# Retention and two expert layers on one core: the retention slots of the first layer one step later, eight weight tiles converted singly

## The chip, the cores and the metric

The kernel runs on one core of one Trainium2 chip. The time is device microseconds (us) of one execution, given as the median of the runs. The engines are called as in the profile: PE (TensorE, matmuls), PEld (its weight loads), DVE (VectorE), ACT (ScalarE), POOL (GpSimd), SP (SyncE, which here only issues DMAs). A line such as L505 is a line of the kernel before the change.

## The reference

```python
for b in range(nb):                                   # retention, 12 blocks of 64 positions
    intra = einsum('bhic,bhjc->bhij', qb, kb) * Dmask
    intra = einsum('bhij,bhjd->bhid', intra, vb)
    inter = einsum('bhid,bhde->bhie', qb * lam_pow, kv_state)
    out[:, :, sl] = intra + inter
    kv_state = lam_block * kv_state + einsum('bhsd,bhse->bhde', kb * rev_pow, vb)
x = attn_out as 1536 tokens x 512
h = x @ w_in ; g = relu(h)**2 ; x = g @ w_out          # block 0: d_ff 2048
out = (sigmoid(x @ w_gate) * (x @ w_val)) @ w_out      # block 1: d_ff 1536
```

q, k, v and lam are float32, the five weight matrices are float64 in memory. Retention has 2 sequences of 768 positions, 8 heads of 64.

## The kernel before, in words

Retention works on chunks of 128 positions: 12 chunks, taken in pairs of one chunk of each sequence, (0, 6), (1, 7), up to (5, 11). Two pairs are done ahead of everything else. They give the first 512 tokens, with which block 0 starts at once; the other four pairs are worked into block 0, while it runs on the first 512 tokens, and give the other 1024 tokens, which block 0 handles afterwards.

**Block 0 on the first 512 tokens** has 16 steps, f = 0 to 15, one for each 128 rows of d_ff (`step_1`). A step has two halves on PE: `stage_a` (12 matmuls, L505), which multiplies the tokens by the weight tile in*f*, and `stage_b` (12 matmuls, L519), which multiplies the squared result of the step *before* by the weight tile out*f-1*. Below they are called A*f* and B*f*: PE's order is A0, A1, B0, A2, B1, A3, B2 and so on. Every float32 operand is split into a high and a low part that PE can multiply at full rate, and a product takes three groups of four matmuls: high by high, low by high (of the weights), high by low. So A*f* needs the high part of its weights (whi, ACT, L240) for the first four matmuls and the low part (wlo, DVE, L243) for the next four. The result of A*f* passes ACT three times (relu L536, square L537, high part gh L549) and DVE once (low part gl, L551) before B*f* can use it.

**Weights** come as float64. SP loads the raw words (`raw`, L149, 512 KB); ACT scales the high and the low word in two instructions (L163, L167), DVE shifts and adds (L174, L179), which leaves float32; later ACT and DVE split it (L240, L243), and SP stores the float32 tile to memory for the tokens that come later (L231). The tiles go in the order in0, in1, out0, in2, out1, in3, out2, in4, out3, in5, ... The first `SINGLE` of them are converted one by one (512 columns an instruction); the rest in couples, two tiles to one instruction of DVE and of the split. `PLAN` says what a step issues: "S" splits the next tile or couple, "A" scales, shifts and adds the next one, "a" and "b" are the two halves of such a conversion. The first S of a step stands ahead of stage_b, the rest behind it. A step that is not in the table has "SA". A step in `LATE` issues gl and the low part of its first S behind stage_b.

**Retention inside block 0.** A half step is one stage: half step 2f comes behind A*f*, half step 2f+1 behind B*f-1*. `SLOTS` gives a half step the scores of a chunk (16 matmuls, L360, then two masks on DVE, L386, and on POOL the decayed keys kd, L376, and queries qd, L368) or the output of a pair (96 matmuls, L412, L428, L440, then the state on DVE, L454, two copies to xr on ACT, L464; on POOL tt, L394). `LOADS` gives the half step at which SP is handed the load of a chunk's q and k (a "q" entry, L118 and L123) or k and v (a "v" entry, L127).

The order of each engine is that in which the program issues, and each engine keeps to it. SP is a queue as well: a DMA whose buffer or semaphore isn't free holds those behind it. Instructions that make the low and high parts of the 1024 other tokens (`combine_x`: xch L597, xcl L600, t L613) and of the combined weights (ah L687, al L693) are put at positions near the end of the sixteen steps; behind them PE goes on with L714 for the other 1024 tokens.

Of the kernel before, what the change touches and what calls it, by code (L numbers as in the profile page):

```python
# [14 lines left out]
TB = 512  # L15
WARM = 14
FILL = 10
SINGLE = 6
PLAN = {
    0: "SAaSb", 3: "SASA", 5: "SAA", 7: "SAA", 8: "SAA",  # L20
    10: "SAS", 11: "SS", 12: "S", 13: "", 14: "", 15: "",
}
LATE = (1,)

PAIRS = ((0, 6), (1, 7), (2, 8), (3, 9), (4, 10), (5, 11))
LEAD = 2
SLOTS = {
    3: ("scores", 2), 4: ("scores", 8), 6: ("out", 2),
    8: ("scores", 3), 9: ("scores", 9), 11: ("out", 3),
    13: ("scores", 4), 14: ("scores", 10), 16: ("out", 4),  # L30
    17: ("scores", 5), 18: ("scores", 11), 20: ("out", 5),
}
LOADS = {
    3: "q3", 4: "q10", 5: "v3", 6: "v9", 8: "q4", 9: "q11",
    10: "v4", 11: "v10", 12: "q5", 13: "q12", 14: "v5", 15: "v11",
}

MM = 0.2267
# [5 lines left out]
def retention_moe_kernel(  # L44
# [92 lines left out]
    order_1 += [(1, NF1 - 2, 1), (1, NF1 - 1, 1)]  # L137
    couples = [(key,) for key in order_1[:SINGLE]]
    couples += [tuple(order_1[n : n + 2]) for n in range(SINGLE, len(order_1), 2)]
    to_load = [key for couple in couples for key in couple]  # L140
# [62 lines left out]
    def several(n, name, dt=F32):  # L203
        return double(name, dt) if n == 2 else unit(name, dt).rearrange("p (n c) -> p n c", n=1)
# [13 lines left out]
    def couple_act():  # L218
        run(couple_ops())
# [15 lines left out]
    def couple_split():  # L235
        if not whole_t:
            return []
        keys, w = whole_t.pop(0)
        hi, lo = (several(len(keys), name, F32R) for name in ("whi2", "wlo2"))
        nc.scalar.copy(hi, w)  # L240
        for n, key in enumerate(keys):
            split_t[key] = hi[:, n], lo[:, n]
        return [lambda: nc.vector.tensor_tensor(out=lo, in0=w, in1=hi, op=ALU.subtract)]  # L243

    def weave(a, b):

        for i in range(max(len(a), len(b))):
            for ops in (a, b):
                if i < len(ops):
                    ops[i]()  # L250

    def run(ops):
        weave(ops, [])
# [10 lines left out]
    S = const.tile([P, 2, 4, 64], F32, name="S")  # L264
# [853 lines left out]
    def load(what, eng=nc.sync):  # L1118

        for x in what.split():  # L1120
            if x == "w":
                load_w(1)
            elif x[0] == "q":
                load_qk(int(x[1:]), eng)
            else:
                load_kv(int(x[1:]), eng)
# [34 lines left out]
    def step_1(f):  # L1161

        acc = stage_a(1, f)
        h = 2 * f
        masks = SLOTS.get(h, ("", 0))[0] == "scores"
        after = attend(h)
        gs, ops = split_g(elem(1, f, acc))
        if masks:
            after()
        if f not in LATE:  # L1170
            run(ops)
        if not masks:
            after()
        while rest:
            rest.pop()()
        plan = PLAN.get(f, "SA")
        lo = []
        if plan.startswith("S"):
            lo = couple_split()
            plan = plan[1:]  # L1180
        if f not in LATE:
            run(lo)
        if prev:
            stage_b(*prev.pop())
        after = attend(h + 1)
        if f in LATE:
            after()
            run(ops)
            run(lo)
            after = lambda: None  # L1190
        half_done = []
        for what in plan:
            if what == "S":
                run(couple_split())
            elif what == "a":
                first, second = couple_ops()
                first()
                half_done.append(second)
            elif what == "b":
                half_done.pop()()  # L1200
                run(couple_dve())
            else:
                couple_act()
                after()
                after = lambda: None
                run(couple_dve())
        after()
        prev.append((1, f, gs))
# [19 lines left out]
    T1 = (24 * NF1 - 12) * MM + 8 * SCORES + 4 * REST  # L1228
# [5 lines left out]
    with tc.manual_schedule():  # L1234
        load_lam()
        load("q6", nc.scalar)
        load("q0 q7 v0 v6 w q1 q8 v1 v7 w w w q2 w w q9")
        decays()
        warm_up(WARM)
        new_xr()  # L1240
        first, second = PAIRS[:LEAD]
        for c in first:
            att_scores(c)
        warm_up(FILL)
        for c in first:
            att_keys(c)
        run([op for c in first for op in att_mask(c)])
        att_uv(first)
        couple_act()
        att_state()  # L1250
        run(couple_dve())
        for c in (7, 1, 8):
            query(c)
        decayed()
        att_out(first)
        x_1 = att_x(first)
        for c in second:
            att_scores(c)
        lo_0 = couple_split()
        run([op for c in second for op in att_mask(c)])  # L1260
        run(lo_0)
        run(x_1)
        for c in second:
            att_keys(c)
        att_out(second)
        x_2 = att_x(second)
        couple_act()
        run(x_2)
        run(couple_dve())
        j_2, r_2 = couple_ops()  # L1270
        j_2()
        lo_1 = couple_split()
        r_2()
        shift_2, add_2 = couple_dve()
        shift_2()
        run(lo_1)
        add_2()
        load("v2 v8")
        att_uv(second)
        rest.append(att_state)  # L1280
        for c in (0, 6, 1, 7):
            qk_t.pop(c)
        for c in (0, 6, 1, 7):
            kv_t.pop(c)
        clock[0] = 0.0
        flush()


        keys = [(1, i, 0) for i in range(NF1 // 2)]
        prepare_a(keys[0], T1 - 2.0)  # L1290
        at(T1 - 20.0, lambda: load_a((1, 1, 0)))
        combine_x(1, [T1 + d for d in (-27, -25, -22.5, -20, -17.5, -15, -12.5, -10, -7, -4, -2)])
        for f in range(NF1):
            step_1(f)
        n_out = 24
        for k in range(3):
            at(T2 - 14.0 + k, lambda: load_w(1))
        for k in range(n_out):
            convert(T2 + 1.0 + k * (T3 - T2 - 4.0) / n_out)
        for f in range(NF1):  # L1300
            prepare_out(1, f, T2 + 24 * MM * f)
        uses = [use for i in range(NF1 // 2) for use in pair_in_1(i)]
        strassen(keys, uses, (None, lambda: close(1)))
        xc.clear()
        new_xr()
        for f in range(2):
            at(T3 - 24.0 + f, lambda f=f: load_units(2, f))
        at(T3 - 14.0, lambda: run(split_w(2, 0)))
        pair_out(1)


        for f in range(2, NF2):
            at(T3 + (36 * (f - 1) - 12) * MM - 8.0, lambda f=f: load_units(2, f))
        for k in range(3 * NF2 - n_out):
            convert(T3 + 2.0 + 3.6 * k)
        for i in range(NF2 // 2):
            sum_out_w(i, T4 - 64.0 + 9.0 * i)
        keys = [(2, i, u) for i in range(NF2 // 2) for u in range(2)]
        prepare_a(keys[0], T4)
        at(T4 - 28.0, lambda: combine_a((2, 0, 1)))  # L1320
        at(T4 - 20.0, lambda: load_a((2, 0, 1)))
        combine_x(2, [T4 - 46.0 + 3.5 * k for k in range(11)])
        for f in range(NF2):
            step_2(f)
        T6 = T5 + 6 * STEP
        by_unit_through_dram(1, T5 - 14.0, T5 - 7.0)
        through_dram(2, T5 - 4.0, T5 + 1.5)
        through_dram(3, T5 + 1.0, T5 + 6.5)
        through_dram(4, T5 + 6.0, T5 + 11.5)
        for n, load, pos in (  # L1330
            (0, -21.0, -13.0), (1, -12.0, -1.5), (2, -6.0, 4.0),
            (3, 1.0, 8.8), (4, 6.0, 13.5), (5, 11.0, 18.3),
        ):
            prepare_w(0, n, n, T5 + load, T5 + pos)
        for n, i, load, pos in (
            (0, 5, -12.5, -5.0), (1, 4, -7.5, -1.0), (2, 3, -3.0, 3.5),
            (3, 0, 1.0, 8.0), (4, 2, 6.0, 12.5), (5, 1, 10.0, 15.5),
        ):
            prepare_w(1, n, i, T6 + load, T6 + pos)
        by_unit_through_dram(2, T6 - 7.0, T6 + 5.0)  # L1340
        by_unit_through_dram(1, T6, T6 + 10.2)
        uses = [use for i in range(NF2 // 2) for use in pair_in_2(i)]
        strassen(keys, uses, (None, lambda: close(2)))
        blocks_out()
        flush()
        assert not agenda and not to_conv and not ready
# [62 lines left out]
```

## Time and profile before

| what | us |
|---|---|
| median of 3 runs | 582.85 (581.88 to 585.62) |
| profiled execution | 586.79 |
| its span, first to last instruction | 585.0 |
| PE busy in the span | 573.7 (98%) |
| DVE busy | 444.2 (76%) |
| ACT busy | 349.4 (60%) |
| mean granted TensorE clock | 0.990 of full speed |

The profiled execution is one run with the profiler on, a little slower than the median of the runs without it. The page gives shares of the whole span; what a change in one stage is worth has to be read in that stage. In the timeline a row has the start, the duration, the engine, the line and operation, the tiles, and in brackets how long the engine sat idle ahead of it and who ended that.

### The profile page before, as it was taken

To read this page: it belongs to the slowest core of one execution; us is meant where nothing else is said; L and a number is where in the kernel's file an instruction comes from. 1 tells how busy PE (TensorE), PEld (TensorE's weight loads), DVE (VectorE), ACT (ScalarE), POOL (GpSimd) and SP (SyncE) were. 2 spreads that over 40 slices of the span, in tenths; PEclk is the share of its full clock that TensorE was granted. 3 is DMA by queue.
4 is the path that set the end of the run, shared out by engine and by line. 5 is a ranking of instruction groups with operands and counts; after the bars stand their busy time and mean duration, and the time that the engine had idled before them with its cause. 6 is when DMAs were issued, how large, how long until landed. Compare 5 with 4: busy or idle time off the path is not lost.

```text
span 585.0 us, 8530 instructions
## 1 busy us (share of the span) xinstructions
PE 573.7 (98%) x3020; PEld 465.1 (79%) x3020; DVE 444.2 (76%) x637; ACT 349.4 (60%) x550; POOL 54.9 (9%) x52
## 2 busy tenths in 40 slices
PE   9988999999999999999999999999999999999996
PEld 5766878888888888888888888888878888878885
DVE  7886787798688866867556778884778877789974
ACT  3656688886465647676448665443554555485470
POOL 4344430000000000000000000012102210000000
PEclk9987999999999999999999999999999999999999
DMA  8998999501444497999994899994547668578671
GB/s 308 408 408 335 319 288 383 180 36 38 143 147 177 162 329 282 408 410 411 403 380 148 289 339 352 363 281 75 155 113 207 193 198 235 169 308 309 210 302 72
DMA packets 69226, 150.25 MB, mean 257 GB/s; under 512 B 6976, under 2 KB 15168, under 8 KB 69184
## 3 DMA queue, kind: packets, MB, share of 16 engines
q1 hardware_dynamic: 65312, 144.86, 68.2%
q0 software_dynamic: 3360, 3.93, 4.4%
q10 hardware_dynamic: 512, 0.92, 0.5%
q8 instruction: 23, 0.38, 0.3%
q14 instruction: 19, 0.16, 0.1%
HBM read 105.91 MB, written 42.21 MB: 253 GB/s over the span
## 4 chain that ended last, share of the span: by engine, by line
PE 87%; DVE 7%; ACT 2%; DMA 2%; issue 1%; DVEq 0%; SPq 0%; ACTq 0%
PE p L714 28%; PE p L505 18%; PE p L1105 15%; PE p L519 12%; PE p L1034 8%; DMA gr<-gs 2%; PE p L360 2%; PE p L440 2%; PE p L324 1%; DVE wlo L243 1%; DVE gq L901 1%; DVE at L386 1%; PE p L412 1%; PE p L428 1%; DVE c L728 1%
## 5 line engine op out<-in xcount | busy, mean ns | idle before, releaser
L714 PE MATMUL p<-xch,ah 128*128 128x512 f32 x280 | 109.9, 392 | 1.0 <-ACT s L723 0.5
L714 PE MATMUL p<-xcl,ah 128*128 128x512 f32 x280 | 109.1, 389 | 0.0
L714 PE MATMUL p<-xch,al 128*128 128x512 f32 x280 | 109.0, 389 | 0.0
L714 PEld LDWEIGHTS p<-xch,ah 128*128 128x128 f32 x280 | 52.5, 188 | 14.9 <-ACT s L723 3.2
L723 ACT COPY s<-p 128x512 f32<-128x512 f32 x60 | 35.1, 588 | 44.3 <-PE p L714 44.2
L714 PEld LDWEIGHTS p<-xch,al 128*128 128x128 f32 x280 | 52.6, 188 | 11.0
L714 PEld LDWEIGHTS p<-xcl,ah 128*128 128x128 f32 x280 | 52.6, 188 | 10.7
L728 DVE TENSOR_TENSOR c<-p,s 128x512 f32<-128x512 f32 x60 | 41.2, 687 | 23.2 <-PE p L714 23.2
L1034 PE MATMUL p<-gq,wq 128*128 128x512 f32 x252 | 57.7, 390 | 1.0 <-DVE wq L991 1.0
L1034 PEld LDWEIGHTS p<-gq,wq 128*128 128x128 f32 x252 | 47.1, 188 | 11.4 <-DVE wq L991 1.7
L163 ACT ACTIVATE j<-raw 128x512 f32<-128x512 f32 x68 | 45.5, 669 | 12.4 <-DMA raw<-in_w 6.6
L179 DVE CUSTOM_DVE_ANT_0 j<-j,r 128x1024 uint16<-128x1024 uint16 (+1 forms) x55 | 48.1, 874 | 6.2 <-DVE j L174 0.5
L1105 PE MATMUL p<-g2l,whi 128*128 128x512 f32 x128 | 49.8, 389 | 0.0
L1105 PE MATMUL p<-g2h,wlo 128*128 128x512 f32 x128 | 49.8, 389 | 0.0
L1105 PE MATMUL p<-g2h,whi 128*128 128x512 f32 x128 | 49.8, 389 | 0.0
L167 ACT ACTIVATE r<-raw 128x512 int32<-128x512 uint32 x68 | 45.1, 663 | 1.5 <-PE p L505 1.0
L505 PE MATMUL p<-xh,wlo 128*128 128x512 f32 x160 | 44.0, 398 | 1.4 <-DVE wlo L243 1.4
L505 PE MATMUL p<-xh,whi 128*128 128x512 f32 x160 | 44.5, 401 | 0.4 <-ACT whi L240 0.4
L505 PE MATMUL p<-xl,whi 128*128 128x512 f32 x160 | 43.6, 395 | 0.0
L662 POOL DMA_DIRECT2D as<-w x6 | 5.6, 926 | 364.3 <-DMA u<-w 292.9
L505 PEld LDWEIGHTS p<-xh,wlo 128*128 128x128 f32 x160 | 30.7, 192 | 8.5 <-DVE wlo L243 1.9
L505 PEld LDWEIGHTS p<-xh,whi 128*128 128x128 f32 x160 | 30.1, 191 | 7.5 <-ACT whi L240 0.8
(126 smaller groups left out, 1026.9 us busy)
## 6 DMA issues: line engine op xcount, KB each, us to landing
raw<-in_w SPq DMA_DIRECT2D x68, 512.0 KB, 7.6
w<-j SPq DMA_DIRECT2D x68, 256.0 KB, 7.3
u<-w SPq DMA_DIRECT2D x52, 256.0 KB, 5.8
a<-w SPq DMA_DIRECT2D x20, 512.0 KB, 4.0
g<-g SPq DMA_DIRECT2D x32, 256.0 KB, 3.7
g<-g SPq DMA_DIRECT2D x16, 512.0 KB, 7.6
kv<-in_kv SPq DMA_DIRECT2D x12, 512.0 KB, 7.9
gr<-gs SPq DMA_DIRECT2D x24, 256.0 KB, 5.5
```

Source lines behind the costliest of these rows:

```text
L163: lambda: nc.scalar.activation(j, t[:, :, 1].bitcast(F32), AF.Prelu, scale=2.0**-80 if flip else 2.0**-112, alpha=2.0**-32 if flip else 2. ...
L167: lambda: nc.scalar.activation(r, low, AF.Copy, scale=2.0**-29),
L179: nc.vector.tensor_tensor(out=j, in0=j, in1=r, op=ALU.add)
L360: nc.tensor.matmul(pv(sc[g])[:, p, :], lhsT=pv(t[:, 1, :])[half(g), p, :], rhs=pv(t[:, 0, :])[half(g), p, :], start=True, stop=True,)
L440: nc.tensor.matmul(ov[s][half(r), p, :], lhsT=v[:, 2 * p + r, :], rhs=pv(at[:, r ^ s, :])[:, p, :], start=n == 0 and p == 0, stop=p == 3, ...
L505: nc.tensor.matmul(acc, lhsT=a[:, kk * P : (kk + 1) * P], rhs=b[:, kk, :], start=i == 0, stop=i == 11,)
L519: nc.tensor.matmul(acc[e], lhsT=a[:, e * P : (e + 1) * P], rhs=b, start=first and i == 0, stop=last and i == 2,)
L714: nc.tensor.matmul(acc, lhsT=w[:, col, kk * P : (kk + 1) * P], rhs=x[:, kk, :], start=start and i == 0, stop=stop and i == 5, skip_group_c ...
L723: nc.scalar.copy(s, acc)
L728: nc.vector.tensor_tensor(out=c, in0=acc, in1=s, op=ALU.add)
L1034: nc.tensor.matmul(acc[k], lhsT=a[:, wn], rhs=block_of(b, gn), start=first and n == 0, stop=last and n == 3 * len(group) - 1,)
L1105: nc.tensor.matmul(acc[e, t], lhsT=a[:, e * P : (e + 1) * P], rhs=b[:, t, :], start=first and i == 0, stop=last and i == 2,)
```

## The change

Three things are changed. Every retention slot of block 0 stands two half steps (one step) later. The loads of q and v move with them, and those of chunks 2, 8 and 9, which were issued ahead of the steps, are now issued in half steps 0 to 4, so that the raw words of the weights stand ahead of them on SP. Eight weight tiles instead of six are converted singly (out2 and in4 were a couple), for which step 2 now has the two conversions that step 0 has, and the table of the other steps is moved by about one step. `LATE` is gone: step 1 issues its instructions as every other step does.

```diff
-SINGLE = 6
+SINGLE = 8
 PLAN = {
-    0: "SAaSb", 3: "SASA", 5: "SAA", 7: "SAA", 8: "SAA",
-    10: "SAS", 11: "SS", 12: "S", 13: "", 14: "", 15: "",
+    0: "SAaSb", 2: "SAaSb", 4: "SASA", 6: "SAA", 9: "SAA",
+    11: "SAS", 12: "SS", 13: "", 14: "", 15: "",
 }
-LATE = (1,)
...
 SLOTS = {
-    3: ("scores", 2), 4: ("scores", 8), 6: ("out", 2),
-    8: ("scores", 3), 9: ("scores", 9), 11: ("out", 3),
...
+    5: ("scores", 2), 6: ("scores", 8), 8: ("out", 2),
+    10: ("scores", 3), 11: ("scores", 9), 13: ("out", 3),
...
 LOADS = {
-    3: "q3", 4: "q10", 5: "v3", 6: "v9", 8: "q4", 9: "q11",
...
+    0: "q2", 1: "q9", 3: "v2", 4: "v8",
+    5: "q3", 6: "q10", 7: "v3", 8: "v9", 10: "q4", 11: "q11",
...
-        if f not in LATE:
-            run(ops)
+        run(ops)
...
-        load("q0 q7 v0 v6 w q1 q8 v1 v7 w w w q2 w w q9")
+        load("q0 q7 v0 v6 w q1 q8 v1 v7 w w w w w")
...
-        load("v2 v8")
...
-        combine_x(1, [T1 + d for d in (-27, -25, -22.5, -20, -17.5, -15, -12.5, -10, -7, -4, -2)])
+        combine_x(1, [T1 + d for d in (-24, -22.5, -20.5, -18.5, -16, -13.5, -11, -8.5, -6, -3.5, -1)])
```

PE, from the end of B0 on, before the change (L360 scores of chunk 2 and 8, L505 A2 and A3, L519 B1, L412 the first matmuls of the output of pair (2, 8); the numbers behind whi and wlo only tell tiles apart):

```order
L360 MATMUL p<-qk 128x128 x8
L505 MATMUL p<-xh,whi_413 128x512 x4
L505 MATMUL p<-xh,wlo_414 128x512 x4
L505 MATMUL p<-xl,whi_413 128x512 x4
L360 MATMUL p<-qk 128x128 x8
L519 MATMUL p<-gh,whi_440 128x512 x4
L519 MATMUL p<-gh,wlo_441 128x512 x4
L519 MATMUL p<-gl,whi_440 128x512 x4
L505 MATMUL p<-xh,whi_531 128x512 x4
L505 MATMUL p<-xh,wlo_532 128x512 x4
L505 MATMUL p<-xl,whi_531 128x512 x4
L412 MATMUL p<-kv,kd 64x64 x16
```

The same place of PE now:

```order
L505 MATMUL p<-xh,whi_409 128x512 x4
L505 MATMUL p<-xh,wlo_410 128x512 x4
L505 MATMUL p<-xl,whi_409 128x512 x4
L519 MATMUL p<-gh,whi_437 128x512 x4
L519 MATMUL p<-gh,wlo_438 128x512 x4
L519 MATMUL p<-gl,whi_437 128x512 x4
L360 MATMUL p<-qk 128x128 x8
L505 MATMUL p<-xh,whi_490 128x512 x4
L505 MATMUL p<-xh,wlo_491 128x512 x4
L505 MATMUL p<-xl,whi_490 128x512 x4
L360 MATMUL p<-qk 128x128 x8
L519 MATMUL p<-gh,whi_541 128x512 x4
```

Both scores stand one step later, and the output of pair (2, 8), which came behind A3, now comes behind A4.

DVE, from the addition for out1 on, before (L386 the masks of a chunk, L551 gl of a step, L243 the low part of a weight tile, L174 and L179 shift and addition):

```order
L179 ISA j_408<-j_408,r_409 128x1024
L386 TENSOR_TENSOR at<-p,D 128x512 x2
L551 TENSOR_TENSOR gl<-g,gh 128x512
L243 TENSOR_TENSOR wlo_441<-j_408,whi_440 128x512
L174 TENSOR_SCALAR j_480<-j_480 128x512
L179 ISA j_480<-j_480,r_481 128x1024
L386 TENSOR_TENSOR at<-p,D 128x512 x2
L551 TENSOR_TENSOR gl<-g,gh 128x512
L243 TENSOR_TENSOR wlo_532<-j_480,whi_531 128x512
```

The same place of DVE now:

```order
L179 ISA j_404<-j_404,r_405 128x1024
L551 TENSOR_TENSOR gl<-g,gh 128x512
L243 TENSOR_TENSOR wlo_438<-j_404,whi_437 128x512
L174 TENSOR_SCALAR j_459<-j_459 128x512
L179 ISA j_459<-j_459,r_460 128x1024
L551 TENSOR_TENSOR gl<-g,gh 128x512
L243 TENSOR_TENSOR wlo_491<-j_459,whi_490 128x512
L386 TENSOR_TENSOR at<-p,D 128x512 x2
L174 TENSOR_SCALAR j_521<-j_521 128x512
L179 ISA j_521<-j_521,r_522 128x1024
L243 TENSOR_TENSOR wlo_542<-j_521,whi_541 128x512
```

The masks leave their place ahead of the conversion of in3 (j_480, now j_459) and stand behind its low part; behind them comes the single conversion of out2 (j_521).

SP, from the raw words of in1 on, before (L118 and L123 q and k of chunks 2 and 9, later 3 and 10, L127 k and v of chunks 2 and 8, L231 the first store):

```order
L149 DMA raw<-in_w 128x1024 x3
L118 DMA qk<-in_qk 128x1024
L149 DMA raw<-in_w 128x1024 x2
L123 DMA qk<-in_qk 128x1024
L149 DMA raw<-in_w 128x1024 x3
L127 DMA kv<-in_kv 128x1024 x2
L149 DMA raw<-in_w 128x1024 x2
L118 DMA qk<-in_qk 128x1024
L149 DMA raw<-in_w 128x1024
L123 DMA qk<-in_qk 128x1024
L231 DMA w_1_72<-j_222 128x512
```

The same place of SP now:

```order
L149 DMA raw<-in_w 128x1024 x8
L118 DMA qk<-in_qk 128x1024
L123 DMA qk<-in_qk 128x1024
L149 DMA raw<-in_w 128x1024 x2
L127 DMA kv<-in_kv 128x1024
L149 DMA raw<-in_w 128x1024
L127 DMA kv<-in_kv 128x1024
L231 DMA w_1_72<-j_218 128x512
```

Counted from the first of these rows, the load of chunk 2's k and v was the 11th DMA and is the 13th; chunk 8's was the 12th and is the 15th; q and k of chunk 2 were the 4th and are the 9th.

## Rows read from the trace of the kernel before

**Rows 1.** The page, part 2: granted TensorE clock in 40 slices of 14.6 us.

```profile
PEclk9987999999999999999999999999999999999999
```

**Rows 2.** Chain of waits, first and last piece of a stretch of PE alone.

```profile
59.20 1.09 PE p L360 x16
...
138.65 2.72 PE p L519 x12
```

**Rows 3.** Timeline of PE, steps 2 to 4.

```profile
29.10 1.16 PE L360 MATMUL p<-qk 64*128 64x128 f32 x16
30.19 1.19 PE L505 MATMUL p<-xh,whi 128*128 128x512 f32 x4
...
33.14 1.16 PE L360 MATMUL p<-qk 64*128 64x128 f32 x16
...
37.61 1.19 PE L505 MATMUL p<-xh,whi 128*128 128x512 f32 x4 [0.35 <-ACT whi L240]
40.25 1.80 PE L505 MATMUL p<-xh,wlo 128*128 128x512 f32 x4 [1.45 <-DVE wlo L243]
...
43.69 1.28 PE L412 MATMUL p<-kv,kd 128*64 128x64 f32 x32
...
49.53 1.19 PE L519 MATMUL p<-gh,whi 128*128 128x512 f32 x4 [1.63 <-ACT whi L240]
51.50 2.07 PE L519 MATMUL p<-gh,wlo 128*128 128x512 f32 x4 [0.77 <-DVE wlo L243]
...
55.08 1.91 PE L505 MATMUL p<-xh,whi 128*128 128x512 f32 x4
```

**Rows 4.** Busy time by stretch: us, PE, PEld, DVE, ACT, POOL, PEclk, DMA share, GB/s.

```profile
40.50:44.00 3.50, 3.50 (x14) 2.34 (x15) 1.52 (x2) 0.20 (x1) 0.00 (x0) 0.51 1.09 416
...
50.50:58.00 7.50, 6.73 (x17) 5.11 (x17) 5.62 (x6) 4.57 (x8) 1.84 (x1) 0.54 0.74 295
```

**Rows 5.** Timeline of ACT, steps 1 to 3.

```profile
31.22 0.62 ACT L240 CAST whi<-j 128x512 fp32r<-128x512 f32 x1
...
32.31 0.66 ACT L167 ACTIVATE r<-raw 128x512 int32<-128x512 uint32 x1
33.25 0.60 ACT L536 ACTIVATE r<-p 128x512 f32<-128x512 f32 x1 [0.28 <-PE p L505]
...
34.54 0.62 ACT L549 CAST gh<-g 128x512 fp32r<-128x512 f32 x1
...
48.43 1.05 ACT L240 CAST whi<-j 128x1024 fp32r<-128x1024 f32 x1
```

**Rows 6.** Timeline of DVE and of POOL, steps 1 to 3.

```profile
29.53 0.42 DVE L174 TENSOR_SCALAR j<-j 128x512 int32<-128x512 int32 x1
30.09 0.69 DVE L179 CUSTOM_DVE_ANT_0 j<-j,r 128x1024 uint16<-128x1024 uint16 x1
...
31.89 0.68 DVE L551 TENSOR_TENSOR gl<-g,gh 128x512 fp32r<-128x512 f32 x1
32.20 1.28 POOL L376 TENSOR_TENSOR kd<-kv,W 128x512 f32<-128x512 f32 x1 [12.80 <-DMA kv<-in_kv]
...
32.49 1.53 DVE L243 TENSOR_TENSOR wlo<-j,whi 128x512 fp32r<-128x512 f32 x1
...
33.95 1.50 DVE L174 TENSOR_SCALAR j<-j 128x512 int32<-128x512 int32 x1
...
36.82 1.28 DVE L386 TENSOR_TENSOR at<-p,D 128x512 f32<-128x512 f32 x2
...
38.00 1.05 POOL L394 TENSOR_TENSOR tt<-S,G 128x512 f32<-128x512 f32 x1
...
45.19 1.27 POOL L368 TENSOR_TENSOR qd<-qk,L 128x512 f32<-128x512 f32 x1
```

**Rows 7.** Timeline of SP's queue: the first five stores.

```profile
30.85 5.44 SPq L231 DMA_DIRECT2D w<-j  x5
```

**Rows 8.** Waits of ACT, 12 to 141 us: total, times, longest.

```profile
ACT j L163 <- DMA raw<-in_w: 6.1, 1, 6.1
```

**Rows 9.** Timeline at the end of the sixteen steps.

```profile
135.86 1.22 DVE L693 TENSOR_TENSOR al<-as,ah 128x1024 fp32r<-128x1024 f32 x1
...
141.20 0.39 PE L714 MATMUL p<-xch,ah 128*128 128x512 f32 x1
```

More of the change, by code (lines that the diff above doesn't have):

```diff
@@ L27 @@
 SLOTS = {
-    3: ("scores", 2), 4: ("scores", 8), 6: ("out", 2),
-    8: ("scores", 3), 9: ("scores", 9), 11: ("out", 3),
-    13: ("scores", 4), 14: ("scores", 10), 16: ("out", 4),
-    17: ("scores", 5), 18: ("scores", 11), 20: ("out", 5),
+    5: ("scores", 2), 6: ("scores", 8), 8: ("out", 2),
+    10: ("scores", 3), 11: ("scores", 9), 13: ("out", 3),
+    15: ("scores", 4), 16: ("scores", 10), 18: ("out", 4),
+    19: ("scores", 5), 20: ("scores", 11), 22: ("out", 5),
 }
 LOADS = {
-    3: "q3", 4: "q10", 5: "v3", 6: "v9", 8: "q4", 9: "q11",
-    10: "v4", 11: "v10", 12: "q5", 13: "q12", 14: "v5", 15: "v11",
[3 rows of a table added]
 }
@@ L1176, in step_1 @@
         plan = PLAN.get(f, "SA")
-        lo = []
         if plan.startswith("S"):
-            lo = couple_split()
+            run(couple_split())
             plan = plan[1:]
-        if f not in LATE:
-            run(lo)
         if prev:
@@ L1185, in step_1 @@
         after = attend(h + 1)
[L1186 to L1190, printed above, removed]
         half_done = []
```

1 row of the table LOADS is left out of this document.

## The prediction

> **What bounds the kernel now.** The page comes first: PE is busy for 98% of the span, and the granted clock falls only in slices 3 and 4 [rows 1], that is about 29 to 58 us. The chain of waits says the same from the other side: from 59.20 to the last piece of the sixteen steps it holds PE and nothing else [rows 2], so nothing that the change moves behind 59 us can make PE earlier, only later. What can be won lies ahead of that, and the timeline of PE shows it: from 29.10 on PE sat idle for 0.35 and 1.45 us in A3, 1.63 and 0.77 us in B2 [rows 3], 4.2 us in all. Behind the wait of 1.45 us and within B2 the granted clock was 0.51 and 0.54 [rows 4], which is the lower level (1.2 of 2.4 GHz) but for the edges. Its price: the last eight matmuls of A3 took 43.69 - 40.25 = 3.44 us where A2's took 33.14 - 31.23 = 1.91 (30.19 + 1.04 is their start), the last eight of B2 55.08 - 51.50 = 3.58 for 1.91, and A4 59.20 - 55.08 = 4.1 for 2.7 [rows 2, 3]. That is 1.5 + 1.7 + 1.4 = 4.6 us. A change that cured all of it would bring 8.8 us, 1.5% of the time.
>
> Why PE waited is in the timeline of DVE and POOL. From 32.20 to 39.05 POOL does five operations of 1.05 to 1.3 us, and each DVE operation with two inputs in SBUF, or the shift, that meets one stands behind it: wlo 1.53 us and the shift 1.50 where they take about 0.6 and 0.42; the masks, which read PSUM, are not held (1.28 for two) [rows 6]. The two engines take turns. The wait of 1.63 us is another chain: the output of pair (2, 8) ends, the second xr copy runs, then the couple's whi for 1.05 us [rows 5], and B2 needs it.
>
> **The change, part by part.** I carry the clock of the profiled execution on, from the end of B0 at 29.10, up to which the order is the same on all engines.
>
> *Raw words ahead of q and v.* Worth nothing by itself: within 12 to 141 us ACT waited for raw words once, for 6.1 us, ahead of the steps [rows 8]. What it does is to move chunk 2's k and v two places back on SP. Eight DMAs are in flight, so the fourth of the five stores goes out when the thirteenth DMA of the list has landed, and that is now this load: 30.85 + 3 x 1.28 = 34.7 us [rows 7]. (For the order before, the same reckoning gives the second store, 32.1; kd began at 32.20 [rows 6].) Chunk 2's q and k land at about 29.6, five us ahead of their scores. So POOL's five operations begin at 34.7 instead of 32.2.
>
> *Scores one step later.* PE does A2 at 29.10 to 31.8 and needs for B1 the whi of out1, done at 31.84 [rows 5]: B1 31.84 to 34.56, no wait. Scores of chunk 2 take 1.09 [rows 3], to 35.65. On ACT the low word of in3 is done at 32.97, relu follows at once because A2 is over, then square and gh, 1.91 us in all as now (33.25 to 35.16) [rows 5], to 34.85, then whi of in3 to 35.4. On DVE the conversion of in3 is done by 33.8, untouched by POOL. A3 starts at 35.65, against 37.61.
>
> *The turns on DVE and POOL*, with 1.05 for kd and tt, 1.27 for qd, 0.6 for a DVE operation [rows 6]: kd to 35.75, gl of step 2 (ready at 34.87, a tenth of a us too late) to 36.35, qd to 37.6, wlo of in3 to 38.2, kd of chunk 8 to 39.25 beside the masks, to 39.45, qd to 40.5, the shift of out2 to 40.9, tt to 41.95, the addition of out2 to 42.55. Then ACT's whi of out2 to 43.15. If gl wins the first turn instead, every second one swaps and this whi is ready at 42.1.
>
> *PE with that.* A3 does four matmuls to 36.7 and waits for wlo until 38.2, 1.5 us, the wait that it has now. Then eight matmuls to 40.1, or 41.6 at the lower clock, chunk 8's scores to 41.2 or 42.7, and in both cases B2 waits for whi of out2, to 43.2. B2 2.95, to 46.1. A4 needs whi of in4: low word, relu, square, gh and whi behind 43.15 on ACT, 0.55 + 1.9 + 0.6, so 46.2. A4 to 48.95. The output of pair (2, 8) takes 49.53 - 1.63 - 43.69 = 4.2 [rows 3], to 53.15. Then the same chain as now: xr, whi of the couple (now out3 and in5), a wait of 1.63, and **B3 starts at 54.8**.
>
> *The sum.* PE now stands at the point at which B2 stood at 49.53 [rows 3], and has done one step more, 2 x 2.72 = 5.44 us of PE [rows 2]. So 49.53 + 5.44 - 54.8 = **0.2 us** gained; 1.2 us if gl wins the first turn. I take the middle, 0.7 us, since a tenth of a us decides it. The two waits in A3 and ahead of B3 are not removed, they are moved; the single conversion only moves the third, from A3 to B2.
>
> *What is left.* The two tiles converted singly cost one split on ACT and three operations on DVE more, some 0.1 us of start-up each, beside PE. The order of step 1 (gl ahead of stage_b) is in the sum. The last pair is one step closer to the end of the sixteen steps, which puts one conversion more (at most 2 x (0.56 + 0.6) = 2.3 us of DVE [rows 6]) and two xr copies into the last 27 us; the last part that PE needs there, al, ended at 137.1, and PE asks for it 1.4 us behind 141.2 [rows 9]: 5.4 us to spare. Cost taken 0; if that cover is gone, up to 1 us.
>
> The profiled execution took 586.79, the median is 582.85; the gain is set against the median: **582.1**.
>
> **The rivals.**
>
> *POOL out of the way (gain).* If POOL's five operations fall between DVE's, wlo of in3 is done at 36.1 and whi of out2 at 39.2, A3 and B2 don't wait, A4 waits little, to 45.5, the output ends at 49.7 and B3 starts at 51.4: 3.6 us gained, **579.2**. For it: DVE is idle for a us ahead of 34.8. Against: rows 6, where no operation slipped past.
>
> *The clock is spared behind B3 (gain).* B2 and A4 lost 1.7 + 1.4 us to the lower level; if the same waits do not bring it back, 0.7 + 3.1 are gained, **579.0**, and with the first rival about 576. The Trainium skill (TensorE: Matmul & The Clock Gate, "HAM oscillation — how this bites in real kernels") puts the fall of the clock down to gaps longer than any wait of this stage; by that rule it would not fall. The trace speaks against it: behind an idle 1.45 us the clock fell at once [rows 3, 4].
>
> *The lower clock comes in B2 (slower).* If the clock holds in A3, PE is idle from 41.2 to 43.2, longer than the wait that brought the lower level before, and with no other work behind it than B2. Twelve matmuls at the rate of 3.58 for eight are 5.4 us instead of 2.95, and nothing hides the 2.4 us, since A4's whi is ready by then. B3 starts at 57.2 (56.2 with gl first): 1.7 us slower, **584.5**, and 3.0, 585.9, if A4 is caught as well. It decides when the wait ahead of B2 is the longer one of the two.
>
> *Nothing arrives.* The steps are paced by ACT and DVE, the wait just moves and the end comes out the same to 0.3 us: 582.9.
>
> **How the numbers follow.** About 1%, 5.8 us, is what a measurement can tell from no change. Chances: the forecast 0.43, POOL out of the way 0.20, the clock spared 0.10, both 0.06, the lower clock in B2 0.17, nothing 0.04. Only both together pass 1% (577.0), with a little from either alone: faster 0.07. Slower by over 1% would take a second stretch of lower clock, or the spare time at the end gone as well: 0.03. The range leaves out the double gain and the worst slow end, and takes in a us of spread of the medians: 577.8 to 585.8. The forecast's own range, by its two orders on DVE, the end and the spread, is 580.5 to 583.5.
>
> **What would show it.** Right: A3 starts near 35.7 and waits some 1.5 us for wlo; kd begins near 34.7; B2 waits for whi near 42 to 43; B3 starts near 54 to 55 behind a wait of about 1.6 us, then the lower clock; no wait of PE from there to L714, which begins within a us of 141.2. Wrong: B3 at 51 to 52 with POOL clear of DVE, clock at full level behind B3, B2 twice as long as 2.95, or a wait of PE near 135 to 143.

## The result and the profile after

The changed kernel takes **586.41 us** (median of 10 runs, 585.98 to 589.11) against 582.94 (581.88 to 585.91) for the kernel before, run beside it: ratio 1.0059 [1.0038, 1.0080]. That is 0.6% slower, outside the range that was forecast.

A number is needed to read all that follows. Each run has a mean granted TensorE clock, and it varies between executions of one and the same kernel. Of 78 runs of the kernel before that were made beside the experiments, 36 had 0.9985 or more and took 581.3 to 583.2, median **581.90**; four had 0.990 or 0.991 and took 586.4 to 587.5. The profiled execution on which the prediction rests (0.990, 586.79) was one like those four; the profiler is not what made it slow, since a second profile of the same kernel, below, took 582.0. Of the ten runs of the changed kernel seven had 0.9985 or more, median 586.05. So without the lower clock the change costs 586.05 - 581.90 = **4.1 us**; the medians, which take in runs with some lower clock, say 3.5. Below, "at full clock" is the median of the runs with 0.9985 or more, against 581.90 (581.7 to 582.0 on the three chips that these 78 runs come from).

The page of the changed kernel shows the granted clock at full level over the whole opening, and a dip in the last slice alone [rows 1]:

```profile
PEclk9999999999999999999999999999999999999998
```

The busy time by stretch (columns as in [rows 4]) puts figures to it:

```profile
40.50:44.00 3.50, 3.12 (x12) 2.10 (x12) 3.33 (x4) 2.73 (x6) 1.93 (x2) 1.00 1.03 403
50.50:58.00 7.50, 5.24 (x45) 4.07 (x42) 4.51 (x5) 4.83 (x8) 3.27 (x3) 1.00 1.03 408
...
572.50:577.00 4.50, 4.45 (x13) 3.52 (x14) 0.69 (x1) 0.59 (x1) 0.00 (x0) 0.62 0.00 0
```

The clock was 1.00 where it had been 0.51 and 0.54 [rows 4]. The dip at 572.5 belongs to the profiled execution (588.42, clock 0.997): 4.5 us at 0.62 are up to 1.7 of the 2 us by which that stands above the median, and nothing of why the median rose.

PE of the changed kernel, the rows that answer to [rows 3], and behind them the end of the sixteen steps [rows 9]:

```profile
35.88 1.20 PE L505 MATMUL p<-xh,whi 128*128 128x512 f32 x4
36.92 1.20 PE L505 MATMUL p<-xh,wlo 128*128 128x512 f32 x4
...
40.55 1.19 PE L519 MATMUL p<-gh,whi 128*128 128x512 f32 x4 [0.42 <-ACT whi L240]
...
44.25 1.20 PE L505 MATMUL p<-xh,whi 128*128 128x512 f32 x4 [0.57 <-ACT whi L240]
46.00 1.19 PE L505 MATMUL p<-xh,wlo 128*128 128x512 f32 x4 [0.55 <-DVE wlo L243]
...
53.76 1.19 PE L519 MATMUL p<-gh,whi 128*128 128x512 f32 x4 [1.63 <-ACT whi L240]
55.59 1.19 PE L519 MATMUL p<-gh,wlo 128*128 128x512 f32 x4 [0.63 <-DVE wlo L243]
...
137.55 0.39 PE L714 MATMUL p<-xch,ah 128*128 128x512 f32 x1
...
145.34 0.50 PE L714 MATMUL p<-xch,ah 128*128 128x512 f32 x1 [0.83 <-ACT s L723]
...
147.78 0.50 PE L714 MATMUL p<-xch,ah 128*128 128x512 f32 x1 [0.77 <-ACT s L723]
```

A3 starts at 35.88 and doesn't wait; the waits now stand at B2 (0.42), A4 (0.57, 0.55) and B3 (1.63, 0.63), and there are two new ones, at 145.34 and 147.78, for s, the copies of L723.

Who won the first turn is seen on POOL and DVE of the changed kernel [rows 6]:

```profile
34.73 1.59 POOL L376 TENSOR_TENSOR kd<-kv,W 128x512 f32<-128x512 f32 x1 [15.43 <-DMA kv<-in_kv]
...
34.73 0.69 DVE L551 TENSOR_TENSOR gl<-g,gh 128x512 fp32r<-128x512 f32 x1 [0.93 <-ACT gh L549]
35.33 1.53 DVE L243 TENSOR_TENSOR wlo<-j,whi 128x512 fp32r<-128x512 f32 x1
```

Both became ready at 34.73; gl took its 0.69, and kd, stretched to 1.59, stood behind it.

### The profile page after: what moved, and what is told of

It reads as the page before. It is cut to its first block, busy times and chain, and to the rows that moved or that the text cites. A ratio compares the mean times of both kernels' runs of the same rounds, so it can differ in the third digit from the quotient of the medians.

```text
span 586.6 us, 8535 instructions
## 1 busy us (share of the span) xinstructions
PE 573.0 (98%) x3020; PEld 462.4 (79%) x3020; DVE 442.0 (75%) x640; ACT 349.3 (60%) x551; POOL 53.4 (9%) x52
## 4 chain that ended last, share of the span: by engine, by line
PE 73%; DVE 10%; ACT 7%; DMA 5%; issue 3%; DVEq 0%; SPq 0%; ACTq 0%
PE p L714 25%; PE p L505 15%; PE p L1105 15%; PE p L519 9%; DMA gr<-gs 4%; PE p L1034 3%; PE p L360 2%; PE p L440 2%; DVE gq L901 2%; PE p L324 1%; DMA D<-wt 1%; DVE wlo L243 1%; ACT ah L687 1%; DVE xcl L600 1%; ACT whi L240 1%
## 5 line engine op out<-in xcount | busy, mean ns | idle before, releaser
L714 PE MATMUL p<-xch,ah 128*128 128x512 f32 x280 | 110.2, 394 | 2.9 <-ACT s L723 2.4
L714 PE MATMUL p<-xcl,ah 128*128 128x512 f32 x280 | 109.1, 389 | 0.0
L714 PE MATMUL p<-xch,al 128*128 128x512 f32 x280 | 109.0, 389 | 0.0
L714 PEld LDWEIGHTS p<-xch,ah 128*128 128x128 f32 x280 | 52.5, 188 | 17.7 <-ACT s L723 6.2
L1034 PE MATMUL p<-gq,wq 128*128 128x512 f32 x252 | 59.8, 399 | 1.6 <-DVE wq L991 1.1
L714 PEld LDWEIGHTS p<-xch,al 128*128 128x128 f32 x280 | 52.6, 188 | 11.0
L723 ACT COPY s<-p 128x512 f32<-128x512 f32 x60 | 35.2, 589 | 43.4 <-PE p L714 43.3
L714 PEld LDWEIGHTS p<-xcl,ah 128*128 128x128 f32 x280 | 52.6, 188 | 10.6
L179 DVE CUSTOM_DVE_ANT_0 j<-j,r 128x1024 uint16<-128x1024 uint16 (+1 forms) x56 | 48.3, 862 | 6.0
L505 PE MATMUL p<-xh,whi 128*128 128x512 f32 x160 | 43.7, 395 | 0.6 <-ACT whi L240 0.6
L505 PE MATMUL p<-xh,wlo 128*128 128x512 f32 x160 | 43.1, 391 | 0.6 <-DVE wlo L243 0.6
L505 PE MATMUL p<-xl,whi 128*128 128x512 f32 x160 | 42.8, 389 | 0.0
L505 PEld LDWEIGHTS p<-xh,wlo 128*128 128x128 f32 x160 | 29.9, 188 | 7.5 <-DVE wlo L243 1.3
L505 PEld LDWEIGHTS p<-xh,whi 128*128 128x128 f32 x160 | 29.4, 188 | 7.6 <-ACT whi L240 1.2
```

Of the source, the lines that this page charges most:

```text
L179: nc.vector.tensor_tensor(out=j, in0=j, in1=r, op=ALU.add)
L505: nc.tensor.matmul(acc, lhsT=a[:, kk * P : (kk + 1) * P], rhs=b[:, kk, :], start=i == 0, stop=i == 11,)
L714: nc.tensor.matmul(acc, lhsT=w[:, col, kk * P : (kk + 1) * P], rhs=x[:, kk, :], start=start and i == 0, stop=stop and i == 5, skip_group_c ...
L723: nc.scalar.copy(s, acc)
L1034: nc.tensor.matmul(acc[k], lhsT=a[:, wn], rhs=block_of(b, gn), start=first and n == 0, stop=last and n == 3 * len(group) - 1,)
```

## The experiments

| | median of its runs | ratio to before | at full clock, against 581.90 |
|---|---|---|---|
| changed kernel | 586.41 | 1.0059 [1.0038, 1.0080] | +4.1 |
| before, again | 582.52 | 0.9996 [0.9974, 1.0017] | +0.3 |
| before, late end | 584.27 | 1.0031 [1.0016, 1.0046] | +2.1 |
| before, places alone | 586.33 | 1.0034 [1.0016, 1.0053] | +2.8 (4 runs) |
| changed opening, old end | 584.25 | 1.0032 [1.0022, 1.0043] | +2.2 |
| changed, old places | 587.49 | 1.0071 [1.0049, 1.0092] | +5.5 |
| before, split first | 581.54 | 0.9963 [0.9944, 0.9983] | -1.2 (2 runs) |
| changed, split first | 584.79 | 1.0015 [0.9999, 1.0031] | +2.9 |
| changed opening, old end, split first | 582.30 | 0.9974 [0.9952, 0.9996] | +0.4 |
| before, split first, v of chunks 2 and 8 later | **578.23** | **0.9898 [0.9878, 0.9919]** | **-3.8** |

The ratios are to runs of the kernel before beside them on the same chip; there were three such groups, with medians of 582.77, 584.09 and 583.16.

**The kernel before, again.** No edit.

> The kernel before, unchanged, with a new profile. Theory (the profile that the prediction used was an execution with the lower clock between 40.5 and 58 us, and most executions have none there): granted clock 1.00 in that stretch, the first L714 at 136.5 to 137.5 us instead of 141.2, an execution of about 582 us instead of 586.8. Rival (the lower clock is there in every execution, and the change really won 4 us by it): clock about 0.5 there again, first L714 near 141. Either way the ratio is 1.000 within 0.003.

Its profile was of an execution with clock 1.000 (582.0). Its busy time by stretch and its PE:

```profile
40.50:44.00 3.50, 3.50 (x68) 2.87 (x70) 1.43 (x2) 1.64 (x3) 0.00 (x0) 1.00 1.04 418
50.50:58.00 7.50, 7.50 (x46) 5.75 (x44) 5.62 (x6) 5.12 (x9) 3.19 (x2) 1.00 1.01 400
```

```profile
40.15 1.20 PE L505 MATMUL p<-xh,wlo 128*128 128x512 f32 x4 [1.45 <-DVE wlo L243]
...
47.90 1.19 PE L519 MATMUL p<-gh,whi 128*128 128x512 f32 x4 [1.63 <-ACT whi L240]
49.16 1.20 PE L519 MATMUL p<-gh,wlo 128*128 128x512 f32 x4
...
135.98 0.39 PE L714 MATMUL p<-xch,ah 128*128 128x512 f32 x1
```

The same waits of 1.45 and 1.63 us stand in it, yet the clock was 1.00 in both stretches. B2 starts at 47.90 and not at 49.53 [rows 3], L714 at 135.98 and not at 141.20 [rows 9]. The 4.6 us that the prediction read as a price of the opening belong to that execution and those like it, not to the waits as such.

**The end alone, in two ways.** First the last pair one step later, with its loads and the new places of `combine_x`, all else as before:

```diff
-    17: ("scores", 5), 18: ("scores", 11), 20: ("out", 5),
+    19: ("scores", 5), 20: ("scores", 11), 22: ("out", 5),
...
-    10: "v4", 11: "v10", 12: "q5", 13: "q12", 14: "v5", 15: "v11",
+    10: "v4", 11: "v10", 14: "q5", 15: "q12", 16: "v5", 17: "v11",
...
-        combine_x(1, [T1 + d for d in (-27, -25, -22.5, -20, -17.5, -15, -12.5, -10, -7, -4, -2)])
+        combine_x(1, [T1 + d for d in (-24, -22.5, -20.5, -18.5, -16, -13.5, -11, -8.5, -6, -3.5, -1)])
```

> The kernel before, with only the last pair moved: scores 5 and 11 and the output of (5, 11) one step later, their loads too, and combine_x at the changed kernel's places; the opening as before. Theory (the loss is made at the end of the sixteen steps, where DVE and ACT reach the first product of the combined weights late): 2.5 to 3.5 us slower than before, 585.4 to 586.4, with waits of PE for ACT's s (L723) in the first key of L714. Rival (the loss is made in the opening, by the singles and the moved scores): within 0.5 us of before.

2.1 us slower, less than the 2.5 to 3.5 expected, for a step that the prediction had priced at 0. The two waits for s stand in its profile (0.54 and 0.79 us). That execution (586.89, clock 0.993) had the lower level behind a wait of 1.40 us in A3:

```profile
40.16 1.70 PE L505 MATMUL p<-xh,wlo 128*128 128x512 f32 x4 [1.40 <-DVE wlo L243]
...
40.50:44.00 3.50, 3.50 (x18) 2.36 (x18) 1.43 (x2) 0.40 (x1) 0.00 (x0) 0.52 1.04 423
```

Then the new places alone (the last two lines of that diff):

> The kernel before, with only combine_x at the changed kernel's later places; the last pair where it was. Theory A (the loss at the end comes from the later places, which put xcl and the sums of the next key behind PE): 1.5 to 2 us slower, as with the last pair moved as well. Theory B (it comes from the last pair's output, one step later, which the copies have to wait for): within 0.4 us of before.

The places alone cost as much (ratio 1.0034 for 1.0031; at full clock 2.8 us, from four runs), and the two waits are there with no slot moved. PE of this kernel:

```profile
144.42 0.50 PE L714 MATMUL p<-xch,ah 128*128 128x512 f32 x1 [0.78 <-ACT s L723]
...
146.85 0.50 PE L714 MATMUL p<-xch,ah 128*128 128x512 f32 x1 [0.79 <-ACT s L723]
```

How the places make s late is seen on ACT and DVE, behind one another as one chain. The kernel before, again:

```profile
134.05 1.22 DVE L613 TENSOR_TENSOR t<-xr,t 128x1024 f32<-128x1024 f32 x1
...
135.30 1.05 ACT L597 CAST xch<-t 128x1024 fp32r<-128x1024 f32 x1
...
139.11 1.05 ACT L687 CAST ah<-as 128x1024 fp32r<-128x1024 f32 x1 [0.98 <-DVE as L681]
140.07 0.58 ACT L723 COPY s<-p 128x512 f32<-128x512 f32 x1
```

The changed kernel:

```profile
138.69 1.22 DVE L613 TENSOR_TENSOR t<-xr,t 128x1024 f32<-128x1024 f32 x1
...
131.79 1.05 ACT L597 CAST xch<-t 128x1024 fp32r<-128x1024 f32 x1 [2.00 <-DVE t L613]
...
139.95 1.05 ACT L597 CAST xch<-t 128x1024 fp32r<-128x1024 f32 x1 [2.54 <-DVE t L613]
...
143.76 1.05 ACT L687 CAST ah<-as 128x1024 fp32r<-128x1024 f32 x1 [1.54 <-DVE as L681]
144.71 0.58 ACT L723 COPY s<-p 128x512 f32<-128x512 f32 x1
```

With later places the last t of `combine_x` ends 4.6 us later, its high part xch waits 2.54 us for it on ACT, the low part xcl follows on DVE, then the sums (L678 to L681), then ah, and behind ah on ACT stand the copies s, which take PE's results out of p. PE, which needs p again, idles 0.83 and 0.77 us. The row at which the prediction had looked, al [rows 9], is not in this chain.

**The opening alone.** The changed kernel with the later pairs and their loads, the plan of later steps and the places of `combine_x` put back (the diff is cut):

```diff
-    0: "SAaSb", 2: "SAaSb", 4: "SASA", 6: "SAA", 9: "SAA",
-    11: "SAS", 12: "SS", 13: "", 14: "", 15: "",
+    0: "SAaSb", 2: "SAaSb", 4: "SASA", 6: "SAA", 7: "SAA", 8: "SAA",
+    10: "SAS", 11: "SS", 12: "S", 13: "", 14: "", 15: "",
...
-    10: ("scores", 3), 11: ("scores", 9), 13: ("out", 3),
+    9: ("scores", 3), 10: ("scores", 9), 12: ("out", 3),
...
-    19: ("scores", 5), 20: ("scores", 11), 22: ("out", 5),
+    17: ("scores", 5), 18: ("scores", 11), 20: ("out", 5),
...
```

> The changed kernel with the last three pairs, their loads, combine_x and the end of the plan brought back to where they stood before (pair (3, 9) one half step later than before), the opening as in the change. Theory (loss at the end, opening about equal): 582 to 583.5 us, that is from 0.5 slower to 1 faster than before, and no wait for s in the first key. Rival (loss in the opening): 586, as the changed kernel.

2.2 us slower, where about as fast as before was expected; the two waits for s are gone from its profile, as expected. In that profile kd won the first turn, by 0.16 us, so that both orders named in the prediction have now been seen. Its POOL, DVE and PE, and its granted clock by stretch:

```profile
34.63 1.04 POOL L376 TENSOR_TENSOR kd<-kv,W 128x512 f32<-128x512 f32 x1 [15.26 <-DMA kv<-in_kv]
...
34.79 1.43 DVE L551 TENSOR_TENSOR gl<-g,gh 128x512 fp32r<-128x512 f32 x1 [0.93 <-ACT gh L549]
...
37.98 1.20 PE L505 MATMUL p<-xh,wlo 128*128 128x512 f32 x4 [0.85 <-DVE wlo L243]
...
42.68 1.19 PE L519 MATMUL p<-gh,whi 128*128 128x512 f32 x4 [1.49 <-ACT whi L240]
...
54.73 1.20 PE L519 MATMUL p<-gh,whi 128*128 128x512 f32 x4 [1.63 <-ACT whi L240]
...
65.19 1.21 PE L519 MATMUL p<-gh,whi 128*128 128x512 f32 x4 [0.36 <-ACT whi L240]
...
139.77 0.39 PE L714 MATMUL p<-xch,ah 128*128 128x512 f32 x1
```

```profile
50.50:58.00 7.50, 5.78 (x70) 4.41 (x63) 2.55 (x3) 4.89 (x8) 4.27 (x4) 0.90 1.03 410
58.00:65.00 7.00, 6.83 (x48) 4.98 (x46) 3.11 (x4) 0.91 (x1) 0.00 (x0) 0.86 0.39 150
```

B3 starts at 54.73; forecast for this order was 54.8. A step takes 5.44 us, so B2 of the kernel before, clean, stands at 47.90 + 5.44 = 53.34 on this scale. The opening loses 1.4 us with kd first and 53.76 - 53.34 = 0.4 with gl first; a wait of 0.63 for wlo behind it makes 1.0 of the latter. Of what is left to 2.2, a wait for whi ten us later is 0.36. The whole agrees with the profile, too: L714 starts 3.8 us behind the clean 135.98, and the lower clock behind B3 (0.90 and 0.86) is at most 0.10 x 7.5 + 0.14 x 7.0 = 1.7 of these, which leaves 2.1. The opening moves the slots, converts two more tiles singly and drops `LATE`; which of the three the loss belongs to, no run separates.

**Old places under the changed kernel.** The theory was that the places are the whole price of the end, and that packing them closer behind the late last pair takes the waits for s away.

```diff
-        combine_x(1, [T1 + d for d in (-24, -22.5, -20.5, -18.5, -16, -13.5, -11, -8.5, -6, -3.5, -1)])
+        combine_x(1, [T1 + d for d in (-24, -23.5, -22.5, -20, -17.5, -15, -12.5, -10, -7, -4, -2)])
```

> The changed kernel, with all but the first three of combine_x's pieces at the places of the kernel before (the first three as early as the last pair's output allows); slots, loads, plan as in the change. Theory (what is lost at the end is the order in which the later places put ACT's xch and the relu of steps 14 and 15, not the last pair's later output): 1.5 to 2.5 us faster than the changed kernel, 0.15% to 0.35% slower than before, and the waits for s in the first key of L714 are back at about 0.5 us in all. Rival (the last pair's step is what DVE and ACT cannot take in): as the changed kernel, 0.5% to 0.6% slower than before.

That theory fell: 587.49, slower than the change itself. PE now waits in the last steps:

```profile
127.29 1.20 PE L519 MATMUL p<-gl,whi 128*128 128x512 f32 x4 [1.08 <-DVE gl L551]
...
132.21 1.20 PE L519 MATMUL p<-gh,whi 128*128 128x512 f32 x4 [0.99 <-ACT gh L549]
...
150.05 0.50 PE L714 MATMUL p<-xch,ah 128*128 128x512 f32 x1 [0.77 <-ACT s L723]
```

The squared result of a step stands behind the conversions of `combine_x`, and one of the two waits for s is still there. With the last pair a step later neither placement that was tried is free: spread out they delay s, packed they delay g and still s. So the later places are enough to make the loss of the end, and with the late pair packing them is no way out; whether a third placement is free, no run shows.

**Split first.** In the chain of 1.63 us, which both kernels have, the couple's whi stands on ACT behind the two xr copies, which wait for PE. Here the retention of that step is issued behind the split. For the kernel before:

```diff
-        if not masks:
+        if not masks and f != 3:
             after()
...
             run(lo)
+        if f == 3:
+            after()
```

> The kernel before, with one order changed: in step 3 ACT makes the couple's whi ahead of the two xr copies (and DVE its wlo ahead of the state), so B2 doesn't wait for the end of the output of pair (2, 8). Theory (the wait of 1.63 us ahead of B2, and of B3 in the changed kernel, is the chain output, xr copy, whi): the wait goes and 1.4 to 1.8 us are gained, 581.2 to 581.5. Rival (the couple's conversion is not ready any earlier, or the next wait takes it up): under 0.5 us.

And the changed kernel, and the changed opening with the old end, with the same edit for step 4 (`f != 4` and `f == 4`):

> The changed kernel, with whi of the couple ahead of the xr copies in step 4. Theory (the same chain stands ahead of B3 there): the wait of 1.63 us goes, but what is won is met at the end of the sixteen steps by DVE and ACT, which are late there already: 0.3 to 1.0 us gained, 585.4 to 586.1. Rival (the end follows PE): 1.6 us gained, 584.8.

> The changed opening with the old end (as in the run with the last three pairs brought back), and whi of the couple ahead of the xr copies in step 4. Theory (the opening of the change keeps the waits ahead of A3, B2 and A4 and only loses the 1.63 us): 0.0% to 0.15% faster than before, so 4 us behind the kernel with the two later loads and the old slots. Rival (the moved slots pay as soon as that wait is gone): 0.5% or more faster than before.

All three gain: 1.2, 1.3 and 1.8 us at full clock over the kernel without the edit. On ACT of the kernel before with it, whi no longer waits for the copies, and B2 starts without a wait:

```profile
44.71 1.04 ACT L240 CAST whi<-j 128x1024 fp32r<-128x1024 f32 x1
46.04 0.59 ACT L464 COPY xr<-p 128x512 f32<-128x512 f32 x1 [0.29 <-PE p L440]
...
46.80 1.20 PE L519 MATMUL p<-gh,whi 128*128 128x512 f32 x4
```

In the changed kernel L714 starts at 136.05 instead of 137.55, and the waits for s stay (0.82, 0.78): this edit doesn't touch the price of the end. The first gain, from two runs, is a little under the 1.4 to 1.8 expected; the last two are above what was expected. For the changed kernel the rival was nearer: the median came to 584.79, and 584.8 had been named for an end that follows PE, so what is won in the opening is not lost again at the end. The last one falls in two groups at the same clock, 581.1 to 581.7 and 582.9 to 583.4; the one profile is of the second, with kd first (kd at 34.77 in 1.04 us, gl at 34.79 stretched to 1.57, 1.02 us of waiting for wlo in A3). Whether the first group is the other order no run shows.

**Split first, and the v of chunks 2 and 8 two places later.** One part of the change, the later load of v, on top of the kernel before with the split first. Chunk 2's is the 13th DMA, as in the change; chunk 8's is the 14th, one place ahead of where the change has it:

```diff
-    3: "q3", 4: "q10", 5: "v3", 6: "v9", 8: "q4", 9: "q11",
+    2: "v2 v8", 3: "q3", 4: "q10", 5: "v3", 6: "v9", 8: "q4", 9: "q11",
...
         add_2()
-        load("v2 v8")
```

> The kernel of the run before this one, and the loads of k and v of chunks 2 and 8 two places later on SP, behind two loads of raw words, with the slots where they were. Theory (A3's waits of 0.36 and 1.45 us come from POOL's five operations falling into the conversion of in3; two DMAs later they begin at 34.7 us, when that conversion is over): 1.0 to 1.8 us more are gained, 579.5 to 580.4. Rival (POOL then holds up gl and wlo of the same step, and A3 waits as long, or the output waits for kd): no gain over the run before this one, or a loss of up to 1.5 us.

**578.23, ratio 0.9898**: faster than both kernels. It gained 2.6 us at full clock (3.3 by medians) over the split alone, more than expected. DVE, POOL and PE of it:

```profile
33.70 0.69 DVE L179 CUSTOM_DVE_ANT_0 j<-j,r 128x1024 uint16<-128x1024 uint16 x1
...
34.80 1.04 POOL L376 TENSOR_TENSOR kd<-kv,W 128x512 f32<-128x512 f32 x1 [15.35 <-DMA kv<-in_kv]
...
38.15 1.20 PE L505 MATMUL p<-xh,wlo 128*128 128x512 f32 x4
...
44.20 1.20 PE L519 MATMUL p<-gh,whi 128*128 128x512 f32 x4
...
55.36 1.20 PE L505 MATMUL p<-xh,whi 128*128 128x512 f32 x4 [0.21 <-DVE at L386]
```

The conversion of in3 ends on DVE before POOL begins at 34.80, so A3 runs through, and up to 55 us the timeline lists no wait. B2 starts at 44.20 instead of 47.90: 3.7 us, the 0.36 and 1.45 of A3 and the 1.63 of B2 (3.4), and 0.2 to 0.3 of smaller gaps. It arrives at the end undiminished (-3.8).

## Why the prediction was wrong

**Right: the path through the opening.** kd at 34.7 (34.73; 34.63 with the old end), A3 at 35.65 (35.88), two possible orders of the turns decided by a tenth of a us, B3 at 54.8 or, with 1.0 us more gained, 53.8 (54.73 and 53.76), the chain of 1.63 us unchanged ahead of it. The waits were moved and not removed, as was said. Within it sizes were off. With gl first A3 did not wait for wlo, where 1.5 us was to be the sign of being right, and whi of out2 came at 40.5 and not 42.1, but A4 then waited 1.12 us for whi and wlo of in4, which gave it back. With kd first A3 waited 0.85 and not 1.5, and B2 started at 42.68 and not 43.2, and A4 gave that back too. So it is in part luck that B3 came within 0.1 us. "Worth nothing by itself" was not tested for the raw words that land earlier; the later v that comes with it is worth 2.6 us in the old order of the slots with the split first, which the prediction did not ask.

**Wrong: the point of departure of the sum.** "So 49.53 + 5.44 - 54.8 = 0.2 us gained; 1.2 us if gl wins" counts from B2 at 49.53, which held 1.5 us of lower clock in A3, and "the gain is set against the median" puts it against runs that mostly had none or little of it (36 of the 78 runs had full clock, 33 more had 0.997). From the clean 47.90 the same working gives 53.34 - 54.8 = -1.5 and, with gl first, -0.5: slower in both orders. The experiment on the opening confirms the sign, with 2.2 us at full clock. The profiled execution stood 3.9 us above the median, and the clock rows said where; what it has above the median can't be won against the median. "A change that cured all of it would bring 8.8 us" counts the same 4.6 us: when the waits were cured in the last experiment, 3.8 came.

**Wrong: "Cost taken 0" at the end.** It costs 2.1 to 2.8 us (late end, places alone), where up to 1 us was allowed for. The step looked at what PE reads directly (al) and at the spare time ahead of it. What was late was on ACT: s, queued behind an instruction that waits for DVE. In the profiles PE of the changed kernel lags the clean one by 1.0 us at 131.52 (130.54 there), 1.6 at L714 (137.55 and 135.98) and 3.6 behind the second wait (147.78 and 144.14): with gl first the opening is 1.0 of it and the end 2.6.

**The sum.** Opening 2.2 and end 2.1 are 4.3 us, against 4.1 measured at full clock. The prediction had +0.7 gained and 0 lost.

**The rivals.** *The clock is spared* came true to the letter (clock 1.00 behind B3) and brought little: 36 of the 78 runs of the kernel before had full clock already, and the change is 3.5 us slower by medians for 4.1 at full clock. *The lower clock in B2* did not occur in any profile of the changed opening, though B2 waited up to 1.54 us. The one profile of that opening that has a drop has it behind the 1.63 us ahead of B3, in the kernel with the old end (clock 0.90 in 50.5 to 58). *POOL out of the way* did not occur in the changed order; in the fastest kernel, in the old order of the slots, POOL's work does miss the conversion of in3. *Nothing arrives* fell: what was won at B2 there (3.7) came out at the end (3.8).

**The rule on the clock.** In the kernel before, again, PE idled 1.45 and 1.63 us and the clock stayed at 1.00; in the first profile it was 0.51 behind the same 1.45, in the late end 0.52 behind 1.40. The Trainium skill (TensorE: Matmul & The Clock Gate, "HAM oscillation — how this bites in real kernels") names longer gaps than these for a fall of the clock: the profile of the kernel before, again, agrees with that, the other two don't. What decides between them no run here shows.

## What to carry to other kernels

Before gains are counted, compare the profiled execution's own time and granted clock with the median: time that only that execution lost is no gain, and the point from which a sum starts must be free of it. Where work is moved towards a hand-over between stages, follow each engine's own queue, not only what the bottleneck reads: a copy that stands behind an instruction waiting for a third engine is late with it. A wait that moves with the change is best taken at its cause, here the place of one split on ACT and the moment a load lets POOL start, which gave 1% with two small edits where the shift of all slots lost 0.6%.

## What the runs showed of the hardware

The granted clock differs between executions of the same kernel: waits of about 1.4 us of PE were followed by the lower level (0.51, 0.52) or not at all (1.00), with 4.8 us between the two profiled executions of the kernel before (586.79 and 582.0). Two instructions that started on DVE and POOL within 0.2 us of each other (34.73 and 34.73; 34.79 and 34.63) went in either order, and the later one was stretched from 0.69 to 1.43 us on DVE or from 1.04 to 1.59 on POOL; B3 on PE began 1.0 us apart (53.76 and 54.73) twenty microseconds later.
